# Two linear-attention blocks and two MLPs on one core: layer-norm sums on ScalarE, two denominators' reciprocals on GpSimd, and a reordered start

## The chip, the cores and the metric

The kernel runs on one core of a Trainium2 chip. The core has five engines with instruction streams of their own: TensorE (PE, matmuls; its weight loads, PEld, overlap them), VectorE (DVE), ScalarE (ACT), GpSimd (POOL) and SyncE (SP), which here issues all DMAs. Each engine takes its instructions in order and waits on semaphores for the others. Matmuls write to PSUM, which GpSimd does not read here; all else lies in SBUF. The metric is the device time of one execution in microseconds.

## The reference

Four layers in turn, A, B, A, B, on x of 1 x 2048 x 576 in bfloat16, each with a layer norm ahead and a residual sum behind it. A is linear attention with 32 heads of 18, B an MLP with 4608 hidden units and a layer norm of its own. Both As share one set of weights, and both Bs another.

```python
def _A_ref(x, wqkv, wo):                       # H = 32, Dh = 18
    q, k, v = split(x @ wqkv)
    phi = lambda t: jnp.where(t > 0, t + 1, jnp.exp(t)) + 1e-6
    pq, pk = phi(q), phi(k)
    kv = jnp.einsum("bhsd,bhse->bhde", pk, v)
    z = jnp.einsum("bhsd->bhd", pk)
    num = jnp.einsum("bhqd,bhde->bhqe", pq, kv)
    den = jnp.einsum("bhqd,bhd->bhq", pq, z)[..., None] + 1e-6
    return merge_heads(num / den) @ wo

def _B_ref(x, w1, b1, w2, b2):
    h = _gelu(_layernorm(x) @ w1 + b1)
    return h @ w2 + b2

x = x + _A_ref(_layernorm(x), wqkv, wo)
x = x + _B_ref(_layernorm(x), w1, b1, w2, b2)
x = x + _A_ref(_layernorm(x), wqkv, wo)
x = x + _B_ref(_layernorm(x), w1, b1, w2, b2)
```

## The kernel before

The 2048 tokens are 16 tiles of 128 rows. All weights stay in SBUF. x travels between layers through DRAM (x_d) in float32. The program is written against a framework that places the semaphores and puts each engine's instructions in an order of its own, near that of the program; matmuls are chained by hand (`pe`), and the first tiles' DVE and ACT work too (`chain_on`).

*Layer norm.* Statistics are two `bn_stats` and one `bn_aggr` on DVE (L278 to L284; L804 and L809 for the first tiles), a small DVE operation gives u = var + eps, or for a B layer, whose two norms are folded into one, var (1 + eps) + eps^2 (L289, L292), and GpSimd raises it to -0.5 (L298, L813). The normalized row y goes into a ring of six buffers and is transposed into yT by TensorE or by a transposing DMA (L365). `LNPipe` takes a tile through these stages, one stage at each `tick`.

*Start (`first_tiles`, L788).* Tiles 0 to 5 of the first layer are ordered by hand: rows are fetched (`load_x0`), normalized (0 to 3 on DVE, L820; 4 and 5 on GpSimd, L824 and L826), transposed on TensorE and projected to k (`k_half`). SP issues the transfers in the order of L177 to L187: rows of tiles 0 and 1, the first half of K's weights, tile 2, the second half, tiles 3, 4, 5, then Q's weights and the rest. Later weights are "late pieces", which the k loop issues by a table (`piece_count`, L238): V's weights (`load_wqkv(2)`) and wo come ahead of w1 and w2.

*Layer A, k loop (L523).* For each tile: k projection and phi (`phi_parts`: exp and identity on ACT, min and max on DVE), ky = y^T phi(k) accumulated over all tiles in six PSUM banks (`ky_acc`), and one or two query projections (`q_proj`, one for each of 5 head groups and 4 chunks of 512 tokens, 20 in all, in the order of `q_left`). After the loop: z (L546), kv = Wv^T ky (L558), and kvwo = kv wo by head group (`kv_wo`), with the last six query projections between. The last projection's phi is held back behind kvwo (`late_phi`).

*Layer A, output tiles (L642).* The numerator is never formed alone: phi(q) is scaled by 1/den and multiplied by kvwo. For each chunk `den_stage` forms the 128x128 denominators in PSUM, takes the reciprocal on DVE (L598) and spreads it with a mask into quad_rden (L600); `scale_stage` broadcasts it to the rows of a head group by a matmul (rden_ps, L606), copies it out of PSUM on ACT (rden_bc, L608) and multiplies phi(q) in place on DVE (L609). Chunks 0 and 1 have their denominators ahead of the loop; those of chunks 2 and 3 are formed after tiles 1 and 4. A chunk is scaled during the four tiles ahead of it. `wo_stage` is ten matmuls for each tile into one of two PSUM buffers (wo_ps, accA and accB in turn), and `residual` adds x on DVE (L442) and stores the row (L448); for tiles 2 and 3 ACT copies the matmul's result out (L439) and GpSimd adds (L440). Tiles 0 to 3 are fed to `LNPipe` at once, since the MLP's first chunk needs them: their norm runs on GpSimd (L302, L313, L323), their transposition by DMA.

*Layer B.* For each chunk of 512 tokens: h = gelu(y w1 + b1) (L718 matmuls in pairs on the upper and lower half of the rows, L714 evictions), then four tiles of h w2 (L765), with the norms of the next chunk or layer in between.

Of the kernel before, what the change touches and what calls it, by code (L numbers as in the profile page):

```python
# [15 lines left out]
P = 128  # L16
# [15 lines left out]
C1 = 1.0 + 1e-6  # L32


def build(tc, A_x, A_wqkv, A_wo, B_w1, B_b1, B_w2, B_b2, out, dbg=None, n_layers=4):
    nc = tc.nc
    dbg = dbg or {}
    with ExitStack() as ctx:
# [5 lines left out]
        bank_turn = dict(n=0, both=True)  # L44
# [14 lines left out]
        nc.gpsimd.memset(neg_half[:], -0.5)  # L59
        pow_warm = const.tile([P, 1], F32, name="pow_warm")  # L60
# [117 lines left out]
        load_x0(1)  # L178
        load_wqkv(1, 0)
        load_x0(2)  # L180
        load_wqkv(1, 1)
        load_x0(3)
# [45 lines left out]
        def bias_turn():  # L228
# [6 lines left out]
        late_pieces = [piece_b1_dma, lambda: load_wqkv(2), piece_wo, w1_left[0], w1_left[1], w1_left[2],  # L235
                       lambda: piece_tail(0), w1_left[3], w1_left[4], lambda: piece_tail(1)] + w1_left[5:] + \
                      [(lambda i=i: piece_w2(i)) for i in range(6)]
        piece_count = {4: 1, 5: 2, 6: 1, 7: 2, 8: 1, 9: 1, 12: 2, 14: 3}  # L238
# [6 lines left out]
        class LNPipe:  # L245
# [3 lines left out]
            def feed(self, xt, t, kind, norm_eng, evac_eng="dve", load_from=None, after=None, agg_after=None,  # L249
                     keep=False):  # L250
                xbar = evac_eng == "xbar"
                self.items.append(dict(stage=(0 if load_from is None else -1), xt=xt, t=t, kind=kind,
                                       norm=norm_eng, evac=evac_eng, load=load_from,
                                       after=after, xbar=xbar, agg_after=agg_after, keep=keep))
# [4 lines left out]
            def tick(self, transposes=1):  # L259
                for it in list(self.items):  # L260
# [7 lines left out]
                    if st == -1:  # L268
# [5 lines left out]
                        it["xt"] = xn  # L274
                    elif st == 0:
# [20 lines left out]
                    elif st == 1:  # L296
                        rstd = work.tile([P, 1], F32, name="ln_rstd", bufs=6)
                        nc.gpsimd.tensor_tensor(out=rstd[:], in0=it["u"][:], in1=neg_half[:], op=ALU.pow)  # L298
                        it["rstd"] = rstd
                    elif st == 2 and it["norm"] != "dve":  # L300
                        nmr = work.tile([P, 1], F32, name="ln_nmr", bufs=4)
                        nc.gpsimd.tensor_scalar(out=nmr[:], in0=it["mv"][:, 0:1], scalar1=-1.0,  # L302
                                                scalar2=it["rstd"][:, 0:1], op0=ALU.mult, op1=ALU.mult)
                        it["nmr"] = nmr
                    elif st in (2, 3):
                        y = y_ring[state["ycnt"] % NY]
                        state["ycnt"] += 1
# [125 lines left out]
        def residual(li, t, halves, on_pool=False):  # L433
            xo = xo_of.pop((li, t))
            last = (li == n_layers - 1)
            xn = work.tile([P, D], F32, name="xn", tag="xn", bufs=5)
            res = xn[:, 0:HALF].bitcast(BF16) if last else xn[:]
            if on_pool:
                nc.scalar.copy(out=res.rearrange("p (h n) -> p h n", h=2), in_=halves)  # L439
                nc.gpsimd.tensor_tensor(out=res, in0=res, in1=xo, op=ALU.add)  # L440
            else:
                total = nc.vector.tensor_tensor(out=res.rearrange("p (h n) -> p h n", h=2), in0=halves,  # L442
                                                in1=xo.rearrange("p (h n) -> p h n", h=2), op=ALU.add)
                dve_last["sum"] = total.ins.name
            if last:
                nc.sync.dma_start(out=out_f[t * P:(t + 1) * P, :], in_=res)
                return None
            nc.sync.dma_start(out=x_d[t], in_=xn[:])  # L448
            return xn

        def layer_A(li, next_kind, pre_a1=None, first_tiles=None):
# [62 lines left out]
            if li > 0:  # L514
                for t in range(3):
                    y_load(t)
                begin, q_at = 0, {t: 1 for t in range(14)}
            else:
                first_tiles(k_half, ky_acc)
                begin, q_at = 5, {t: 1 + (t in (12, 14)) for t in range(4, NT)}  # L520
                ky_acc(3, range(KD))
                q_proj(*q_left.pop(0))
            for t in range(begin, NT):  # L523
                if li > 0 and t + 3 < NT:
                    y_load(t + 3)
                k_proj(t, 0)
                if t in q_at and t >= 1:
                    ky_acc(t - 1, range(KD - 1))
                k_proj(t, 1)
                pre_a1(t)  # L530
                if t >= 1:
                    ky_acc(t - 1, (KD - 1,) if t in q_at else range(KD))
                for _ in range(q_at.get(t, 0)):
                    q_proj(*q_left.pop(0))
# [51 lines left out]
            def den_stage(c):  # L586
                dp = bank([P, 512], F32, "den_ps")
                for g in range(G):
                    for j in range(TPC):
                        pe(nc.tensor.matmul(dp[32 * j:32 * (j + 1), 0:P], lhsT=zsel[0:GR[g], g, :],  # L590
                                         rhs=pq[(g, c)][0:GR[g], j * P:(j + 1) * P],
                                         start=(g == 0), stop=False))
                for j in range(TPC):
                    pe(nc.tensor.matmul(dp[32 * j:32 * (j + 1), 0:P], lhsT=eps_row[:], rhs=one_row[:],
                                        start=False, stop=True))
                rden = work.tile([P, P], BF16, name="rden", bufs=1)
                with nc.allow_low_precision("reciprocal of the denominator in the reference's bfloat16"):
                    nc.vector.reciprocal(out=rden[:], in_=dp[:, 0:P])  # L598
                quad = blk.tile([P, D], BF16, name="quad_rden", tag="blk")
                nc.vector.tensor_tensor(out=quad[:, 0:CA].rearrange("p (j n) -> p j n", j=4), in0=quad_mask[:],  # L600
                                        in1=rden[:].unsqueeze(1).to_broadcast([P, 4, P]), op=ALU.mult)
                quad_rden[c] = quad
# [9 lines left out]
            def wo_stage(t):  # L612
                c, j = divmod(t, TPC)
                wp = ps_acc.tile([P, 2, 512], F32, name="wo_ps", tag=("accA", "accB")[t % 2])
                for half in range(2):
                    for g in range(G):
                        pe(nc.tensor.matmul(wp[:, half, 0:HALF], lhsT=pq[(g, c)][0:GR[g], j * P:(j + 1) * P],  # L617
                                              rhs=kvwo[g][0:GR[g], half * HALF:(half + 1) * HALF],
                                              start=(g == 0), stop=(g == G - 1)))
                xn = residual(li, t, wp[:, :, 0:HALF], on_pool=t in (2, 3))  # L620
                if xn is not None and next_kind == "B" and t < TPC:
                    lnp.feed(xn, t, "B", "pool", "xbar")
# [18 lines left out]
            late_phi(after=dve_last["kvwo"], act_after=act_last["kvwo"])  # L641
            for t in range(NT):  # L642
# [3 lines left out]
                wo_stage(t)  # L646
# [9 lines left out]
                if t == NT - 3:  # L656
                    warm_table(ACT.Gelu_apprx_tanh, act_last["copy"])
                lnp.tick()
# [129 lines left out]
        def first_tiles(k_half, ky_acc):  # L788
            ln = {}

            def dve(inst):
                chain_on("dve", inst)
                return inst
# [21 lines left out]
            def norm(t, engine):  # L815
                it = ln[t]
                y = y_of[t] = y_ring[state["ycnt"] % NY]
                state["ycnt"] += 1
                if engine == "dve":
                    dve(nc.vector.tensor_scalar(out=y[:, 0:D], in0=it["x"][:], scalar1=it["mv"][:, 0:1],  # L820
                                                scalar2=it["rstd"][:, 0:1], op0=ALU.subtract, op1=ALU.mult))
                else:
                    nmr = work.tile([P, 1], F32, name="ln_nmr", bufs=4)
                    nc.gpsimd.tensor_scalar(out=nmr[:], in0=it["mv"][:, 0:1], scalar1=-1.0,  # L824
                                            scalar2=it["rstd"][:, 0:1], op0=ALU.mult, op1=ALU.mult)
                    last = nc.gpsimd.tensor_scalar(out=y[:, 0:D], in0=it["x"][:], scalar1=it["rstd"][:, 0:1],  # L826
                                                   scalar2=nmr[:], op0=ALU.mult, op1=ALU.add)
                    pool_last["norm"] = last.ins.name
                del x0_tiles[t]
# [22 lines left out]
            norm(0, "dve")  # L852
# [4 lines left out]
            norm(1, "dve")  # L857
            stats(2, (1,))
            power(2)
            a00, d00 = k_half(0, 0)  # L860
            act(*a00())
            turn(1, False)("dve")
            a01, d01 = k_half(0, 1)
            act(*a01())
            norm(2, "dve")
            a10, d10 = k_half(1, 0)
            stats(3)
            turn(2, True)()
            power(3)
            both(d00())  # L870
            act(*a10())
            a11, d11 = k_half(1, 1)
            act(*a11())
            norm(3, "dve")
# [6 lines left out]
            both(d10())  # L881
# [4 lines left out]
            norm(4, "pool")  # L886
            a30, d30 = k_half(3, 0)
            act(*a30())
            both(d20())
            both(d21())  # L890
# [7 lines left out]
            norm(5, "pool")  # L898
            both(d30())
            both(d31())  # L900
# [21 lines left out]
        for _ in range(4):  # L922
            late_pieces.pop(0)()
# [85 lines left out]
```

## Time and profile before

| | us |
|---|---|
| median of 3 runs (range) | 772.43 (771.15 to 772.85) |
| the profiled execution | 770.18 |
| its span on the core | 768.5 |
| layer 0, first k projection to last output matmul | 6.1 to 106.2 |
| layer 1 (MLP), first matmul to last | 106.2 to 388.1 |
| layer 2, first k projection to last output matmul | 388.1 to 483.1 |
| layer 3 (MLP) and the last store | 483.1 to 768.5 |

How to read the profile: a group has the line of the program, the engine, the operation, written tile <- read tiles, shapes and count, then busy us and the mean ns of one, then how long the engine sat idle just before and what ended that. Positions on the time axis are us from the span's start. A wait names the engine that waited and the instruction whose end released it. In a timeline the figures ahead of an instruction are its start and its duration. "PE busy" counts matmuls from the first to the modelled end, so that back-to-back matmuls of 288 columns show 286 ns each but start every 123 ns.

### The profile page before, as it was taken

How to read it: one execution, taken by the hardware profiler on the slowest of the kernel's cores; microseconds unless marked ns; L12 is line 12 of the kernel's file. 1: busy time of each engine (PE TensorE's matmuls, PEld its weight loads, DVE VectorE, ACT ScalarE, POOL GpSimd, SP SyncE). 2: the span in 40 equal slices, each digit the busy share in tenths (PEclk: the TensorE clock that was granted, in tenths of full speed). 3: DMA queues.
4: the chain of work that ended last, by engine and by line, in shares of the span. 5: the costliest groups of instructions: out<-in, count | busy, mean ns of one | idle time of the engine just before them, and what ended most of it. 6: DMA issues, size and time to landing. Idle time of an engine off the chain costs nothing.

```text
span 768.5 us, 15502 instructions
## 1 busy us (share of the span) xinstructions
PE 755.3 (98%) x6402; PEld 480.4 (63%) x6410; DVE 247.3 (32%) x651; ACT 317.9 (41%) x705; POOL 124.0 (16%) x216
## 2 busy tenths in 40 slices
PE   8999899999999999999999999999999999999998
PEld 4766554675477457646776666447745764674476
DVE  7886952125013402301244589462000000000000
ACT  4667546304600750263056674560065026205600
POOL 3670511013000301200100005321010010011000
PEclk9999999999999999999999999999999999999999
DMA  8979584027113703400431039672100110011000
GB/s 246 216 193 334 149 257 96 28 77 148 35 48 97 142 1 81 126 8 17 133 87 47 9 105 262 212 168 71 49 16 2 32 62 1 25 32 39 2 28 20
DMA packets 82865, 71.13 MB, mean 93 GB/s; under 512 B 44970, under 2 KB 67434, under 8 KB 82794
## 3 DMA queue, kind: packets, MB, share of 16 engines
q1 hardware_dynamic: 82794, 70.14, 33.9%
q8 instruction: 50, 0.82, 0.4%
q14 instruction: 21, 0.17, 0.1%
HBM read 41.74 MB, written 18.87 MB: 79 GB/s over the span
## 4 chain that ended last, share of the span: by engine, by line
PE 93%; DVE 3%; DMA 1%; POOL 1%; issue 1%; ACT 1%; SPq 0%; DVEq 0%; POOLq 0%
PE m_ps L765 37%; PE h_ps L718 20%; PE hp_ps L718 16%; PE q_ps L502 5%; PE ky_ps L491 5%; PE k_ps L461 5%; PE wo_ps L617 4%; DVE pq L609 1%; PE rden_ps L606 1%; DMA x_d<-xn 1%; DMA x<-in_A_x_dram 1%; DVE xn L442 0%; PE kv_ps L558 0%; POOL xn L440 0%; DVE kvwo L580 0%
## 5 line engine op out<-in xcount | busy, mean ns | idle before, releaser
L765 PE MATMUL m_ps<-w_sb,hT 128*128 128x288 bf16 x2304 | 283.6, 286 | 0.0
L765 PEld LDWEIGHTS <-hT 128*128 128x128 bf16 x2304 | 224.8, 98 | 59.8 <-issue 3.4
L718 PEld LDWEIGHTS <-w_sb 64*128 64x128 bf16 x2304 | 124.4, 94 | 136.6 <-issue 1.9
L718 PE MATMUL hp_ps<-yT,w_sb 64*128 64x512 bf16 x1152 | 178.0, 376 | 0.0
L442 DVE TENSOR_TENSOR xn<-m_ps,x_ring 128x576 f32<-128x576 f32 (+1 forms) x32 | 24.2, 758 | 415.4 <-PE m_ps L765 415.4
L718 PE MATMUL h_ps<-yT,w_sb 64*128 64x512 bf16 x1152 | 147.9, 376 | 0.0
L723 ACT COPY relay_sb<-relay_sb 128x1 f32<-128x1 f32 x144 | 28.5, 198 | 264.9 <-PE h_ps L718 222.6
L714 ACT ACTIVATE hT<-h_ps,b1T 128x512 bf16<-128x512 f32 x144 | 91.0, 683 | 44.5 <-PE h_ps L718 44.5
L714 ACT ACTIVATE hT<-hp_ps,b1T 128x512 bf16<-128x512 f32 x144 | 91.1, 692 | 0.0
L426 POOL TENSOR_TENSOR x_ring<-x_ring,b_bc 128x576 f32<-128x576 f32 x32 | 40.7, 1275 | 245.8 <-DMA x_ring<-x_d 243.0
L298 POOL TENSOR_TENSOR ln_rstd<-ln_u,neg_half 128x1 f32<-128x1 f32 x58 | 32.4, 559 | 294.1 <-DVE ln_u L289 201.8
L718 PE MATMUL h_ps<-yT,w_tail 64*128 64x512 bf16 x144 | 54.1, 376 | 0.0
L718 PE MATMUL hp_ps<-yT,w_tail 64*128 64x512 bf16 x144 | 54.1, 376 | 0.0
L461 PE MATMUL k_ps<-wqkv_sb,yT 128*128 128x288 bf16 x320 | 49.2, 286 | 0.9 <-ACT phi_a L396 0.6
L491 PE MATMUL ky_ps<-pk,y_ring 128*128 128x192 bf16 (+5 forms) x318 | 48.7, 285 | 0.5 <-ACT phi_a L396 0.2
L502 PE MATMUL q_ps<-yT,wqkv_sb 128*126 128x512 bf16 (+1 forms) x200 | 48.9, 379 | 0.1
L617 PE MATMUL wo_ps<-kvwo,pq 126*128 126x288 bf16 (+1 forms) x320 | 44.1, 286 | 5.0 <-DVE pq L609 3.1
L393 ACT ACTIVATE phi_e<-k_ps 128x288 bf16<-128x288 f32 x64 | 26.5, 413 | 50.9 <-PE k_ps L461 50.6
L617 PEld LDWEIGHTS <-pq 126*128 126x128 bf16 (+1 forms) x320 | 30.1, 97 | 17.8 <-DVE pq L609 5.1
L461 PEld LDWEIGHTS <-yT 128*128 128x128 bf16 x320 | 30.8, 98 | 14.2 <-issue 1.9
L718 PEld LDWEIGHTS <-w_tail 64*128 64x128 bf16 x288 | 27.1, 94 | 17.1
L400 DVE TENSOR_SCALAR phi_e<-phi_e 128x288 bf16<-128x288 bf16 (+2 forms) x104 | 28.5, 274 | 27.1 <-ACT phi_e L393 26.7
(102 smaller groups left out, 482.7 us busy)
## 6 DMA issues: line engine op xcount, KB each, us to landing
x_ring<-x_d SPq DMA_DIRECT2D x66, 288.0 KB, 3.1
x_d<-xn SPq DMA_DIRECT2D x48, 288.0 KB, 2.6
w_sb<-in_B_w_dram SPq DMA_DIRECT2D x6, 864.0 KB, 10.2
w_sb<-in_B_w_dram SPq DMA_DIRECT2D x9, 512.0 KB, 4.8
x<-in_A_x_dram SPq DMA_DIRECT2D x16, 144.0 KB, 3.6
x_ring<-in_A_x_dram SPq DMA_DIRECT2D x16, 144.0 KB, 3.0
y_d<-y_ring SPq DMA_DIRECT2D x16, 144.0 KB, 1.8
y_ring<-y_d SPq DMA_DIRECT2D x16, 144.0 KB, 2.2
```

What stands on the lines that cost most here:

```text
L298: nc.gpsimd.tensor_tensor(out=rstd[:], in0=it["u"][:], in1=neg_half[:], op=ALU.pow)
L393: exp = nc.scalar.activation(out=e[0:rows, 0:n], in_=ps_ap, func=ACT.Exp)
L400: low = nc.vector.tensor_scalar(out=e[0:rows, 0:n], in0=e[0:rows, 0:n], scalar1=1.0, scalar2=1e-6, op0=ALU.min, op1=ALU.add)
L426: nc.gpsimd.tensor_tensor(out=xo, in0=xo, in1=b2_bc[:], op=ALU.add)
L461: pe(nc.tensor.matmul(kp[:, 0:HALF], lhsT=yT[:, k, tok], rhs=wqkv_sb[:, k, D + half * HALF: D + (half + 1) * HALF], start=(k == 0), stop=( ...
L491: pe(nc.tensor.matmul(ky[at // 512][:, at % 512:at % 512 + n], lhsT=y_of[t][:, c * P:(c + 1) * P], rhs=pk_tiles[t][:, d:d + n], start=(t = ...
L502: pe(nc.tensor.matmul(qp[0:GR[g], :], lhsT=wqkv_sb[:, k, GO[g]:GO[g] + GR[g]], rhs=yT[:, k, c * CA:(c + 1) * CA], start=(k == 0), stop=(k ...
L617: pe(nc.tensor.matmul(wp[:, half, 0:HALF], lhsT=pq[(g, c)][0:GR[g], j * P:(j + 1) * P], rhs=kvwo[g][0:GR[g], half * HALF:(half + 1) * HALF ...
L714: act_last["gelu"] = nc.scalar.activation(out=hT[f][:, 0:CB], in_=dst[n], func=ACT.Gelu_apprx_tanh, bias=b1T[:, f:f + 1], scale=1.0).ins.name
L718: mm = pe(nc.tensor.matmul(dst[n], lhsT=wt, rhs=mv, start=(seen[n] == 0), stop=(seen[n] == 8)))
L723: relay = nc.scalar.copy(out=relay_sb[:, 1:2], in_=relay_sb[:, 0:1])
L765: pe(nc.tensor.matmul(acc[:, half, 0:HALF], lhsT=hT[f][:, j * P:(j + 1) * P], rhs=w2_sb[:, f, half * HALF:(half + 1) * HALF], start=(f == ...
```

## The change

- *Start:* tile 2's rows are fetched ahead of K's weights, tile 3's ahead of their second half. All of tiles 0 to 5 are normalized on DVE, and the DVE, ACT and k-projection steps of the first tiles are set in another order.
- *Late pieces:* w1's first seven column blocks and its tails come first, then V's weights, wo and b1, then the rest.
- *Query projections:* in layer 0 one tile (13) has two of them instead of two tiles (12 and 14), in layer 2 tile 13 has none; in both layers the last one is issued after `late_phi`, just ahead of the output tiles. The ky matmuls are split around the k projection by whether the tile before had a query projection.
- *Residual:* all sums run on DVE; the way over ACT and GpSimd is gone.
- *Statistics of output tiles 0 to 3:* two ACT passes with a running sum take the place of `bn_stats`: Identity with scale -ROOT/D gives minus the mean (times ROOT), Square with that as bias gives the variance. u then comes from GpSimd. These tiles are fed one tile later.
- *Denominators of chunks 2 and 3:* ACT copies them from PSUM to SBUF in float32, and GpSimd raises the 128x128 tile to -1.

The framework's order of the changed kernel differs in the same places; DVE's row among the output tiles becomes: sum 0, phi, sum 1, four scalings of chunk 1, quad_rden of chunk 2, sum 2, last scaling of chunk 1, sums 3 and 4, two scalings of chunk 2, sum 5, quad_rden of chunk 3, scaling, sum 6, two scalings, sums 7 and 8. GpSimd's becomes: power of chunk 2, norms of tiles 0, 1 and 2, power of chunk 3, norm of tile 3.

```diff
+ROOT = D ** -0.5
...
-        bank_turn = dict(n=0, both=True)
+        bank_turn = dict(n=1, both=True)
...
+        minus_one = const.tile([P, 1], F32, name="minus_one")
+        nc.gpsimd.memset(minus_one[:], -1.0)
...
         load_x0(0)
         load_x0(1)
+        load_x0(2)
         load_wqkv(1, 0)
-        load_x0(2)
+        load_x0(3)
         load_wqkv(1, 1)
-        load_x0(3)
...
-        late_pieces = [piece_b1_dma, lambda: load_wqkv(2), piece_wo, w1_left[0], w1_left[1], w1_left[2],
-                       lambda: piece_tail(0), w1_left[3], w1_left[4], lambda: piece_tail(1)] + w1_left[5:] + \
+        late_pieces = w1_left[0:5] + [lambda: piece_tail(0), lambda: piece_tail(1)] + w1_left[5:7] + \
+                      [lambda: load_wqkv(2), piece_wo, piece_b1_dma] + w1_left[7:] + \
                       [(lambda i=i: piece_w2(i)) for i in range(6)]
-        piece_count = {4: 1, 5: 2, 6: 1, 7: 2, 8: 1, 9: 1, 12: 2, 14: 3}
+        piece_count = {4: 1, 5: 1, 6: 1, 7: 2, 8: 1, 9: 1, 12: 2, 13: 1, 14: 3}
...
+                    elif st == 0 and it["stat"] == "act":
+                        xt = it["xt"]
+                        y = it["y"] = y_ring[state["ycnt"] % NY]
+                        state["ycnt"] += 1
+                        mv = work.tile([P, 2], F32, name="ln_mv", bufs=6)
+                        nc.scalar.activation(out=y[:, 0:D], in_=xt[:, 0:D], func=ACT.Identity, scale=-ROOT / D,
+                                             accum_out=mv[:, 0:1])
+                        nc.scalar.activation(out=y[:, 0:D], in_=xt[:, 0:D], func=ACT.Square, scale=ROOT,
+                                             bias=mv[:, 0:1], accum_out=mv[:, 1:2])
+                        it["mv"] = mv
...
                     elif st == 1:
+                        if it["stat"] == "act":
+                            it["u"] = work.tile([P, 1], F32, name="ln_u", bufs=4)
+                            nc.gpsimd.tensor_scalar(out=it["u"][:], in0=it["mv"][:, 1:2], scalar1=1.0 + EPS,
+                                                    scalar2=EPS * EPS, op0=ALU.mult, op1=ALU.add)
...
-        def residual(li, t, halves, on_pool=False):
+        def residual(li, t, halves):
...
-            if on_pool:
-                nc.scalar.copy(out=res.rearrange("p (h n) -> p h n", h=2), in_=halves)
-                nc.gpsimd.tensor_tensor(out=res, in0=res, in1=xo, op=ALU.add)
-            else:
...
-                begin, q_at = 0, {t: 1 for t in range(14)}
+                begin, q_at = 0, {t: 1 for t in range(13)}
...
-                begin, q_at = 5, {t: 1 + (t in (12, 14)) for t in range(4, NT)}
+                begin, q_at = 5, {t: 1 + (t == 13) for t in range(4, NT)}
...
-                if t in q_at and t >= 1:
+                apart = t - 1 in q_at
+                if apart:
                     ky_acc(t - 1, range(KD - 1))
...
-                    nc.vector.reciprocal(out=rden[:], in_=dp[:, 0:P])
+                    if c < 2:
+                        nc.vector.reciprocal(out=rden[:], in_=dp[:, 0:P])
+                    else:
+                        den = blk.tile([P, D], BF16, name="den", tag="blk")[:, 0:2 * P].bitcast(F32)
+                        nc.scalar.copy(out=den, in_=dp[:, 0:P])
+                        nc.gpsimd.tensor_tensor(out=rden[:], in0=den, in1=minus_one[:].to_broadcast([P, P]), op=ALU.pow)
...
-                xn = residual(li, t, wp[:, :, 0:HALF], on_pool=t in (2, 3))
-                if xn is not None and next_kind == "B" and t < TPC:
-                    lnp.feed(xn, t, "B", "pool", "xbar")
+                xn = residual(li, t, wp[:, :, 0:HALF])
+                return xn
...
             late_phi(after=dve_last["kvwo"], act_after=act_last["kvwo"])
+            q_proj(*q_left.pop(0))
+            rows_of = {}
...
-                wo_stage(t)
+                rows_of[t] = wo_stage(t)
...
+                if 1 <= t <= TPC and next_kind == "B":
+                    lnp.feed(rows_of[t - 1], t - 1, "B", "pool", "xbar", stat="act")
                 lnp.tick()
...
-            norm(4, "pool")
...
+            norm(4)
...
-        for _ in range(4):
+        for _ in range(2):
             late_pieces.pop(0)()
```

## The prediction

> **What bounds the kernel now.** I read the shares of the span first, then the engines' busy time by stage, TensorE's waits, and the timelines of the two stretches that are not full.
>
> ```profile
> span 768.5 us, 15502 instructions
> PE 755.3 (98%) x6402; PEld 480.4 (63%) x6410; DVE 247.3 (32%) x651; ACT 317.9 (41%) x705; POOL 124.0 (16%) x216
> PE 93%; DVE 3%; DMA 1%; POOL 1%; issue 1%; ACT 1%; SPq 0%; DVEq 0%; POOLq 0%
> ```
>
> TensorE (PE) is busy 98% and holds 93% of the chain that ended last, so the reader should look only for what fills or opens PE's 13 idle us. By stage (columns: window, its length, then each engine's busy us; layer 0 ends near 106, layer 2 runs from 388 to 483):
>
> ```profile
> 75.00:80.00 5.00, 4.13 (x23) 2.30 (x24) 4.90 (x12) 4.86 (x10) 0.00 (x0) 1.00 0.16 55
> 80.00:106.20 26.20, 24.37 (x218) 16.75 (x221) 22.69 (x50) 10.97 (x20) 11.00 (x18) 1.00 0.78 218
> 106.20:388.00 281.80, 281.80 (x2450) 175.16 (x2450) 64.69 (x151) 99.01 (x218) 38.18 (x61) 1.00 0.32 79
> 458.00:483.00 25.00, 23.14 (x210) 16.18 (x210) 22.09 (x48) 10.84 (x19) 11.24 (x18) 1.00 0.86 261
> ```
>
> The MLP layers have no idle PE at all, at a granted clock of 1.00; nothing in the change can shorten them. VectorE (DVE, third pair) is all but full just where PE is not: 4.90 of 5 us before the output tiles, 22.69 of 26.2 during them. TensorE's waits say on what (us in total, times, longest):
>
> ```profile
> PE wo_ps L617 <- DVE pq L609: 3.1, 2, 1.6
> PE wo_ps L617 <- DVE kvwo L580: 1.6, 2, 0.8
> PE tp L836 <- POOL y_ring L826: 0.7, 1, 0.7
> ```
>
> Both first lines occur once in each attention layer. In layer 0's timeline (start, us, instruction):
>
> ```profile
> 79.00 1.58 PE L617 MATMUL wo_ps<-kvwo,pq 126*128 126x288 bf16 x10 [0.78 <-DVE kvwo L580]
> 85.50 0.87 DVE L600 TENSOR_TENSOR quad_rden<-quad_mask,rden 128x512 bf16<-128x512 bf16 x1
> 86.43 2.68 POOL L440 TENSOR_TENSOR xn<-xn,x_ring 128x576 f32<-128x576 f32 x2
> 86.67 1.31 DVE L609 TENSOR_TENSOR pq<-pq,rden_bc 72x512 bf16<-72x512 bf16 x1
> 88.04 0.91 PE L617 MATMUL wo_ps<-kvwo,pq 72*128 72x288 bf16 x6 [1.52 <-DVE pq L609]
> ```
>
> The scaling at 86.67 takes 1.31 us where its like takes 0.42 (L609 at 83.99), because GpSimd's add runs from 86.43; the quad_rden product takes 0.87 instead of 0.42 beside the normalization on GpSimd from 85.28. A two-input DVE operation stands still until the GpSimd instruction is over. The Trainium skill's page "SBUF — State Buffer" says this as a rule: the port pair that VectorE and GpSimd share is locked for a whole instruction, and the loser waits it out; the trace agrees. By that rule a long GpSimd instruction would also hold every such DVE operation; here none is due during it, as the order below shows.
>
> **The change, part by part.**
>
> *Start-up.* Tile 2's rows are fetched two weight transfers earlier (issue 2.79 becomes about 1.66), tiles 4 and 5 are normalized on DVE (L820, 0.43 us) instead of GpSimd (0.26 + 0.82 plus gaps: 15.47 to 16.66). PE's waits there are 0.59 (tile 1's norm, behind the late rows), 0.72 (tile 4's norm) and 0.24. In the best case all 1.5 go. In the worst the first K weights, issued one row transfer (0.43) later, reach the first projection 0.3 late. I take -0.7: tile 4's wait goes; tile 1's is mostly handed to tile 2, whose norm came at 8.97 behind its GpSimd power and now stands behind two phi operations as well.
>
> *Weights of V and wo later.* They now follow seven pieces of w1, issued about 52 to 54 instead of 14 to 16. They are needed at 69.3 (kv_ps) and 72.6 (kvwo_ps); the same sizes took 5.8 us to land, the slowest weights 10.2. Some 7 us of cover hide it: 0.
>
> *One query projection moved.* From the k loop into the wait before the first output tile. It is 5 x 0.2155 = 1.08 us and the hole 0.78, so that tile starts 0.78 earlier in each layer; in layer 0 one of two steps with a double projection goes, which each ran 4.86 - 3.53 - 1.08 = 0.25 over. Together -1.03 (layer 0) and -0.78 (layer 2). The bounds are 0 (ACT, at 4.86 of 5, holds its phi up) and -1.3.
>
> *The output tiles.* Per layer this takes from DVE two reciprocals (0.95 each) and four tiles' statistics (2 x 0.45 + 0.20 + 0.15 = 1.25), from GpSimd two adds (1.34 each), from ACT two copies (0.64). It adds on DVE two sums (0.75); on ACT eight passes over 128x576 with a running sum (not in this trace; 0.64 is the copy of such a tile, 1.0 the 128x1024 cast of L539; I take 0.72) and two den copies (about 0.3); on GpSimd four small ops (0.26) and two powers over 128x128. PE gets nothing new, so all depends on order. In the changed kernel's instruction order DVE holds, in this row: four scalings of chunk 1, quad_rden of chunk 2 (waits for the power), sum of tile 2, last scaling of chunk 1, sums of tiles 3 and 4, two scalings of chunk 2, sum of tile 5, quad_rden of chunk 3 (waits for the second power), and the rest. So the power does not run beside slack: tile 4's matmuls need sum 2 (two PSUM buffers) and the last scaling, and both are queued behind it.
>
> With P for one power, counted from the first output matmul: it and the ACT chain (sum 0 at 1.35 to 2.1, one statistics pass, four rden copies at 0.52, den copy 0.3) let the first power start at 5.35; quad_rden 0.42 and sum 2 0.76 put tile 4 at 6.7 + P. Before, tile 4 ended at 88.95 - 79.00 = 9.95; now at 6.7 + P + 1.23 = 7.95 + P. GpSimd then holds three normalizations ahead of the second power, each 0.26 + 0.55 + 0.26 + 0.82 + 0.30 and gaps = 2.5, so that starts at 5.35 + P + 7.5 and not when its input is there, some 2.2 earlier. Behind it stand quad_rden, a scaling and sum 6 (0.42 + 0.42 + 0.75), and tile 8 (1.23 plus 0.2) ends at 15.9 + 2P. Before it ended at 96.09 - 79.00 = 17.1 (layer 2: 17.3). So each layer changes by 2P - 1.2 and 2P - 1.4. Tiles 9 to 15 are PE's pace as before, and the last normalization is done 2.5 us after the second power, with eight tiles (about 11 us) before the MLP needs it.
>
> *The price of P.* No power wider than 128x1 is in the trace. The nearest rows on GpSimd (line, form, count, busy us, mean ns):
>
> ```profile
> L426 POOL TENSOR_TENSOR x_ring<-x_ring,b_bc 128x576 f32<-128x576 f32 x32 | 40.7, 1275 | 245.8 <-DMA x_ring<-x_d 243.0 <-DVE ln_st L279 2.8
> L298 POOL TENSOR_TENSOR ln_rstd<-ln_u,neg_half 128x1 f32<-128x1 f32 x58 | 32.4, 559 | 294.1 <-DVE ln_u L289 201.8 <-DVE ln_u L292 92.2
> L824 POOL TENSOR_SCALAR ln_nmr<-ln_mv,ln_rstd 128x1 f32<-128x1 f32 x2 | 0.5, 264 | 0.2
> ```
>
> Lower end: the power's 0.56 stays and 127 more columns go at the add's 1275/576 = 2.2 ns: 0.84 us. Upper end: the power's surplus over a plain 128x1 operation, 0.56 - 0.26 = 0.30, is paid for each of 128 columns: 0.26 + 38 = 38.7 us. The row that is the same operation (L298) says that one column costs 0.30 more than arithmetic, so the add's pace is unlikely; but part of that is paid once and columns may overlap. With ends this far apart I take their geometric middle, sqrt(0.84 x 38.7) = 5.7 us, that is 0.04 us a column.
>
> **The sum.** -0.7 - 1.03 - 0.78 - 1.2 - 1.4 + 4P = 4P - 5.1; with 5.7 it is +17.7. The profiled execution (770.18 us, span 768.5) would become 787.9. It is 2.2 below the shown median of 772.43, to which the same difference gives 790. Break-even is P = 1.28.
>
> **Rivals.** (A) The power streams like the add, P = 0.84: 4 x 0.84 - 5.1 = -1.7, or 770.7, faster. For it: the three other removals are real and DVE is what is full. Against: the 0.30 surplus of a single column. It decides at P = 1.28, and counts up to about 1.7. The Trainium skill's "GPSIMD Engine Reference", section "Performance versus the Vector engine", would have it so for two-input arithmetic: about 2.6 cycles an element at 1.2 GHz, by which an estimate of P is 0.56 + 0.28 = 0.84; the add row's 2.2 ns agrees with that page, and no row shows whether it holds for a power. (B) Columns do not overlap, P from 21 to 38.7: at the end +149.7, or 922. For it: the 0.30. Against: in one instruction some of that is surely paid once. (C) The power is as forecast but PE is not held, since chunk 2's scaled rows are due only after tile 4: then some 2.5 us of each power lie hidden, 17.7 - 10 = +7.7, or 780. Against: sum 2 and the last scaling stand behind quad_rden on DVE, and an engine takes its queue in order.
>
> **How the numbers follow.** Forecast (P between 1.7 and 21, PE held): 0.66, with its own range 774 to 851; A 0.15; B 0.12; C 0.07. The range 771 to 851 leaves out B and the faster part of A, about 2 in 10. This kernel's measurement can tell 0.2%, 1.5 us: faster means P under 0.9, 0.08; the same up to 1.66, 0.08; slower all the rest, 0.84.
>
> **What would show it.** The rows of the 128x128 power on GpSimd give P at once. If the steps hold, the waits list PE wo_ps behind DVE xn (or pq) in four places, two in each attention layer, each near P - 1 us, with DVE idle before quad_rden and GpSimd as releaser, and GpSimd without gaps between its first power and its second; the wait on kvwo is gone, and so is the one of tile 4's transposes; MLP stretches of 281.8 us are as before. I am wrong if P is under 1.3, if PE runs through tile 4 while the power is on, or if a new wait on a weight transfer stands before kv_ps.

## The result and the profile after

| | before | after |
|---|---|---|
| median (range), 4 runs each | 772.19 (771.15 to 772.85) | 851.92 (851.10 to 852.41) |
| span of the profiled execution | 768.5 | 849.8 |
| mean granted clock of TensorE | 1.00 | 0.949 |

The changed kernel takes 1.1033 times as long, with a 95% interval of 1.1014 to 1.1052: some 80 us more. The head of its profile page and the row of the clock that the throttle granted, by slices of a fortieth of the span:

```profile
span 849.8 us, 15505 instructions
...
PE 762.2 (90%) x6406; PEld 484.1 (57%) x6410; DVE 238.7 (28%) x621; ACT 327.9 (39%) x737; POOL 201.8 (24%) x221
...
PEclk9999567999999999999999995599999999999999
```

TensorE's share fell from 98% to 90%, while its busy time rose by 7 us although it has only four matmul records more. GpSimd's busy time rose by 78. The clock row says where: the fives mark two places, one in each attention layer. GpSimd's costliest new group (line, form, count, busy us, mean ns) and TensorE's longest wait (us in total, times, longest):

```profile
L621 POOL TENSOR_TENSOR rden<-den,minus_one 128x128 bf16<-128x128 f32 x4 | 83.1, 20786 | 63.0 <-ACT den L620 63.0
```

```profile
PE wo_ps L640 <- DVE xn L459: 80.9, 4, 20.5
```

One power over 128x128 takes 20.8 us. There are four of them, and four waits of TensorE together nearly as long. The timeline of layer 0 (start, us, instruction; the rows of three engines in order of time) shows how the one leads to the other:

```profile
76.90 1.44 PE L640 MATMUL wo_ps<-kvwo,pq 126*128 126x288 bf16 x10
...
82.13 20.83 POOL L621 TENSOR_TENSOR rden<-den,minus_one 128x128 bf16<-128x128 f32 x1 [28.03 <-ACT den L620]
...
102.99 0.43 DVE L623 TENSOR_TENSOR quad_rden<-quad_mask,rden 128x512 bf16<-128x512 bf16 x1 [20.65 <-POOL rden L621]
...
104.14 2.56 PE L640 MATMUL wo_ps<-kvwo,pq 126*128 126x288 bf16 x10 [20.25 <-DVE xn L459]
...
110.93 20.75 POOL L621 TENSOR_TENSOR rden<-den,minus_one 128x128 bf16<-128x128 f32 x1
...
133.20 2.56 PE L640 MATMUL wo_ps<-kvwo,pq 126*128 126x288 bf16 x10 [20.48 <-DVE xn L459]
...
136.40 2.46 PE L640 MATMUL wo_ps<-kvwo,pq 126*128 126x288 bf16 x10
```

DVE sits idle for 20.65 us ahead of quad_rden, released by GpSimd. TensorE names sum 2 (xn, L459) as its releaser, because that sum stands behind quad_rden in DVE's queue: the name in the wait is the last link, and the cause is one row further up. The second power has no idle time in brackets: GpSimd came to it straight from its three normalizations. The tile behind each wait takes 2.56 us instead of 1.39. By stage (window, length, busy us of PE, PEld, DVE, ACT, POOL, then granted clock, DMA share, GB/s):

```profile
84.00:104.10 20.10, 0.00 (x0) 0.00 (x0) 1.11 (x3) 0.70 (x2) 19.92 (x3) 0.58 0.00 0
...
133.20:147.07 13.87, 13.87 (x86) 9.19 (x87) 8.69 (x16) 4.22 (x7) 1.44 (x3) 0.81 0.57 195
147.07:428.90 281.83, 281.83 (x2450) 175.33 (x2450) 64.69 (x151) 98.98 (x218) 38.28 (x61) 1.00 0.31 79
```

In the first window GpSimd works nearly alone. In the second TensorE is full again, but at a mean clock of 0.81. The MLP lasts 281.8 us as before.

### The profile page after: what moved, and what is told of

It is laid out like the page before. It is cut to its first block, busy times and chain, and to the rows that moved or that the text cites. A ratio compares the mean times of both kernels' runs of the same rounds, so it can differ in the third digit from the quotient of the medians.

```text
span 849.8 us, 15505 instructions
## 1 busy us (share of the span) xinstructions
PE 762.2 (90%) x6406; PEld 484.1 (57%) x6410; DVE 238.7 (28%) x621; ACT 327.9 (39%) x737; POOL 201.8 (24%) x221
## 5 line engine op out<-in xcount | busy, mean ns | idle before, releaser
L459 DVE TENSOR_TENSOR xn<-m_ps,x_ring 128x576 f32<-128x576 f32 (+1 forms) x32 | 24.3, 758 | 415.0 <-PE m_ps L791 415.0
L640 PE MATMUL wo_ps<-kvwo,pq 126*128 126x288 bf16 (+1 forms) x320 | 49.6, 311 | 80.9 <-DVE xn L459 80.9
L447 POOL TENSOR_TENSOR x_ring<-x_ring,b_bc 128x576 f32<-128x576 f32 x32 | 40.7, 1277 | 247.8 <-DMA x_ring<-x_d 242.8
L621 POOL TENSOR_TENSOR rden<-den,minus_one 128x128 bf16<-128x128 f32 x4 | 83.1, 20786 | 63.0 <-ACT den L620 63.0
L640 PEld LDWEIGHTS <-pq 126*128 126x128 bf16 (+1 forms) x320 | 32.9, 104 | 96.1 <-issue 82.8
L631 ACT CAST rden_bc<-rden_ps 126x512 bf16<-126x512 f32 (+1 forms) x40 | 21.4, 588 | 55.4 <-PE rden_ps L629 55.1
```

Of the source, the lines that this page charges most:

```text
L447: nc.gpsimd.tensor_tensor(out=xo, in0=xo, in1=b2_bc[:], op=ALU.add)
L621: nc.gpsimd.tensor_tensor(out=rden[:], in0=den, in1=minus_one[:].to_broadcast([P, P]), op=ALU.pow)
```

## The experiments

Each kernel ran beside the kernel before on the same chip; a ratio is against that. The questions were: what the price of a power consists of, whether TensorE's wait follows it one to one, whether the order on DVE or that on GpSimd sets the wait, what the low clock adds, and what the rest of the change is worth.

**1. The power by itself.** Powers of several shapes and one product on GpSimd are appended to the kernel before, after its last work. Their results are not used, and the time of the whole (824.27 us, one run) is not a comparison.

```diff
+            for n in (2, 8, 32, 64, 128):
+                nc.gpsimd.tensor_tensor(out=low[:, 0:n], in0=src[:, 0:n], in1=minus_one[:].to_broadcast([P, n]),
+                                        op=ALU.pow)
+            nc.gpsimd.tensor_tensor(out=low[0:32, 0:P], in0=src[0:32, 0:P],
+                                    in1=minus_one[0:32, :].to_broadcast([32, P]), op=ALU.pow)
...
+            nc.gpsimd.tensor_tensor(out=low[:, 0:120], in0=src[:, 0:120], in1=minus_one[:].to_broadcast([P, 120]),
+                                    op=ALU.mult)
```

> The kernel before with nine extra GpSimd operations behind its last sum (rows on a constant 3.0, results unused); its time is longer by what they take and is not compared. Theory (each column costs the same, nothing overlaps; 20.8 us for 128 columns and 0.55 for one give 0.159 us a column): 128x2 0.7, 128x8 1.7, 128x32 5.5, 128x64 10.6, 128x128 20.8, 32x128 20.8 (columns count, not partitions), 128x100 to -0.5 in float32 16.3, product 128x120 about 0.5. Rival 1 (the cost is by elements): 32x128 takes 5 us. Rival 2 (the cost hangs on the values or the exponent): 128x128 of the constant is far from 20.8, or 128x100 is not 0.78 of it. Rival 3 (a step with size, as for a buffer): the column price jumps between two of the sizes.

The groups by line of that run (form, count, busy us, mean ns, idle before):

```profile
L953 POOL TENSOR_TENSOR x_ring<-x_ring,minus_one 128x128 bf16<-128x128 f32 x1 | 20.7, 20725 | 0.1
L955 POOL TENSOR_TENSOR x_ring<-x_ring,minus_one 32x128 bf16<-32x128 f32 x1 | 20.7, 20705 | 0.1
...
L953 POOL TENSOR_TENSOR x_ring<-x_ring,minus_one 128x64 bf16<-128x64 f32 x1 | 10.5, 10518 | 0.1
...
L953 POOL TENSOR_TENSOR x_ring<-x_ring,minus_one 128x2 bf16<-128x2 f32 x1 | 0.7, 706 | 0.1
...
L959 POOL TENSOR_TENSOR x_ring<-x_ring,minus_one 128x120 bf16<-128x120 f32 x1 | 0.4, 386 | 0.1
```

From 2 to 128 columns the time grows by 20725 - 706 ns over 126 columns, 0.159 us each, and 0.39 us remains that is paid once. Width 64 by that line is 10.56 (measured 10.52), width 1 is 0.55 (the 128x1 powers of the kernel take 0.56). A quarter of the partitions costs the same. The exponent -0.5 over 128x100 took 16.31, on the line too. A product over 120 columns with the same broadcast operand took 0.386 us in all. So it is the power that is dear, column by column, and neither the broadcast operand nor a wide instruction as such.

**2. The powers taken out.** All reciprocals go back to DVE; all else of the change stays.

```diff
-                    if c < 2:
+                    if c < NCA:
                         nc.vector.reciprocal(out=rden[:], in_=dp[:, 0:P])
```

> The changed kernel with all four chunks' reciprocals on DVE again; all else as changed. Theory (the power is the whole loss, everything else in the change is a gain): PE's four waits of 20 us behind DVE's sum go; the output tiles start 2.1 us (layer 0) and 1.5 us (layer 2) earlier than before, as in the changed kernel's trace, and tiles 0 to 8 run near PE's pace, 14.8 instead of 17.2 us each layer: 772.2 - 3.6 - 4.8 = 764, range 762 to 767. Rival 1 (my prediction's terms without the power, 4 x 0.6 - 5.1): 769.5. Rival 2 (the rest of the change loses too, by the ACT passes with running sums or by the later weights): 772 or more.

Measured: 763.01 us, ratio 0.9895 (0.9879 to 0.9910), clock 0.999. As expected, and faster than both kernels. TensorE's wait on DVE and the window from the first output tile to the MLP in layer 0, in that run:

```profile
PE wo_ps L640 <- DVE xn L459: 0.3, 2, 0.2
```

```profile
76.96:102.46 25.50, 25.23 (x225) 17.45 (x225) 20.53 (x41) 17.13 (x38) 9.52 (x20) 1.00 0.85 270
```

The stretch takes 25.5 us (27.2 before), TensorE is busy for 25.23 of it, and DVE has room. With the reciprocals on DVE there is thus next to nothing left that taking them from DVE could win there: TensorE's waits on DVE's sums are 0.3 us in the whole kernel.

**3. The rest of the change, split.** One kernel has the start, the late pieces and the query projections alone (the statistics, sums and reciprocals are those of before); the other is the kernel of experiment 2 (kernel 2 from here on) with the statistics of tiles 0 to 3 on DVE again, fed at their own tile.

```diff
-                if 1 <= t <= TPC and next_kind == "B":
-                    lnp.feed(rows_of[t - 1], t - 1, "B", "pool", "xbar", stat="act")
+                if t < TPC and next_kind == "B":
+                    lnp.feed(rows_of[t], t, "B", "pool", "xbar")
```

> The kernel before with only the new start, the new order of late weights and the moved query projections; statistics, sums and reciprocals of the output tiles as before. Theory: the output tiles start 2.1 and 1.5 us earlier and then run as before: 772.2 - 3.6 = 768.6, range 767.5 to 770. Rival 1 (the moved projection's phi holds ACT and DVE up and the tiles give it back): 771 to 772. Rival 2 (the prediction's -0.7 -1.03 -0.78): 769.7.

> As e1 (all reciprocals on DVE), and the statistics of output tiles 0 to 3 on DVE again, fed at their own tile; the sums stay on DVE. Theory: DVE is the engine that is full, so its 4 x 1.25 us of statistics in each layer come back into the way of the scalings: about half shows, 767 to 769, that is 3 to 5 above e1 and near e6. Rival (the sums on ACT and GpSimd were the loss, and the statistics fit into DVE's gaps): within 1 us of e1.

Measured: 767.21 us (0.9950, 0.9938 to 0.9963) and 765.45 us (0.9927, 0.9915 to 0.9940). Beside 771.37 for the kernel before, on the same chip as kernel 2, that is a chain of steps: start, pieces and queries -4.2; the sums of tiles 2 and 3 on DVE -1.8; the ACT statistics -2.4; 8.4 in all. The second kernel's expectation was missed from both sides: neither did it fall back to the first, nor did it stay within 1 us of kernel 2. The waits of the first of the two say what the other steps remove:

```profile
PE wo_ps L621 <- DVE pq L613: 3.1, 2, 1.7
...
PE wo_ps L621 <- DVE xn L445: 0.9, 1, 0.9
```

These 4.0 us are 2.6 in the second kernel and 0.3 in kernel 2, and 767.21 - 763.01 is 4.2.

**4. The powers alone.** In the kernel before, only the ACT copy and the power of chunks 2 and 3 are put in.

```diff
+        minus_one = const.tile([P, 1], F32, name="minus_one")
+        nc.gpsimd.memset(minus_one[:], -1.0)
...
-                    nc.vector.reciprocal(out=rden[:], in_=dp[:, 0:P])
+                    if c < 2:
+                        nc.vector.reciprocal(out=rden[:], in_=dp[:, 0:P])
+                    else:
+                        den = blk.tile([P, D], BF16, name="den", tag="blk")[:, 0:2 * P].bitcast(F32)
+                        nc.scalar.copy(out=den, in_=dp[:, 0:P])
+                        nc.gpsimd.tensor_tensor(out=rden[:], in0=den, in1=minus_one[:].to_broadcast([P, P]), op=ALU.pow)
```

> The kernel before with only the den copy and the power for chunks 2 and 3; start, statistics and sums as before. Theory: each of the four powers lengthens the path by 20.8 + 0.3 - 0.95 = 20.1, less the 1.5 us that PE waited at tile 4 anyway, and the low clock behind each wait adds about 2: 772.2 + 80.6 - 3 + 8 = 858, range 852 to 862. Rival (the new statistics on ACT and GpSimd are what holds the second power up, by 2 us a layer): 848 or less.

Measured: 860.89 us, ratio 1.1157 (1.1137 to 1.1176), 88.9 above the 772.00 of the kernel before on its chip. From kernel 2 to the changed kernel the same edit costs 851.92 - 763.01 = 88.9; these two ran on different chips, and with each against the kernel before on its own chip it is 79.7 + 8.4 = 88.1. The loss comes from the powers whatever stands around them; they need no help from the moved statistics and sums.

**5. Half a power.** The power over 64 of the 128 columns, DVE's reciprocal over the others, in the changed kernel.

```diff
+                        n = P // 2
...
+                        nc.vector.reciprocal(out=rden[:, n:P], in_=dp[:, n:P])
+                        nc.gpsimd.tensor_tensor(out=rden[:, 0:n], in0=den, in1=minus_one[:].to_broadcast([P, n]),
+                                                op=ALU.pow)
```

> The changed kernel with GpSimd's power over 64 of the 128 columns of each denominator tile; the other 64 are a DVE reciprocal from PSUM. Theory (the power lies on the path with its whole length, four times): it falls from 20.8 to about 10.5, 851.9 - 4 x 10.3 = 810.7, range 807 to 814. Rival 1 (a part of the power is hidden, so that half of it is hidden more): under 800. Rival 2 (what costs is not the length but the wait as such, PE's clock after it): 830 or more.

Measured: 813.39 us, ratio 1.0532 (1.0514 to 1.0551); one power 10.6 us:

```profile
L623 POOL TENSOR_TENSOR rden<-den,minus_one 128x64 bf16<-128x64 f32 x4 | 42.4, 10605 | 62.2 <-ACT den L621 62.2
```

The time falls by 38.5 where the four powers shrink by 4 x (20.79 - 10.61) = 40.7: TensorE pays for them nearly one to one.

**6. The order on DVE.** The quad_rden products of chunks 2 and 3 are placed behind the sums of tiles 4 and 8, so that tile 4 doesn't wait for a power.

```diff
+                    if c >= 2:
+                        tc.add_manual_dep(prod.ins, dve_last["sum"], NOSYNC, reason="after the sums")
...
+                if t in (4, 8):
+                    quad_rden[1 + t // 4]()
```

> The changed kernel with quad_rden of chunks 2 and 3 put behind the sums of tiles 4 and 8 in DVE's queue (before, ahead of sums 2 and 6). Theory (PE is held by DVE's order, and the second power starts only when GpSimd has done three norms): PE runs through tile 4, the second power starts no earlier after the first, and only tile 8 with its sums comes out from behind the second: 2 to 3 us a layer, 851.9 - 5 = 847, range 844 to 849. Rival 1 (the prediction's rival C, 2.5 us of each power can lie hidden): 842. Rival 2 (the order is no cause): 851 to 853.

Measured: 852.48 us, ratio 1.1046 (1.1030 to 1.1063): nothing won. TensorE's wait moved to the next place that needs the product, and GpSimd's second power starts later (113.65, after 110.93):

```profile
PE rden_ps L638 <- DVE quad_rden L624: 80.3, 4, 22.6
```

```profile
113.65 20.75 POOL L621 TENSOR_TENSOR rden<-den,minus_one 128x128 bf16<-128x128 f32 x1
```

The number is the rival's, but the test isn't clean: in this kernel GpSimd had four normalizations ahead of the second power instead of three, and so lost what tile 4 had gained. What it does show is that DVE's order alone does not free the time while two powers and the normalizations between them stand in one queue.

The same trace answers a question that the prediction left at a rule, namely whether a long GpSimd instruction holds every DVE operation with two inputs in SBUF. Here a scaling became due during the first power:

```profile
82.36 20.83 POOL L621 TENSOR_TENSOR rden<-den,minus_one 128x128 bf16<-128x128 f32 x1 [28.03 <-ACT den L620]
...
84.19 0.42 DVE L641 TENSOR_TENSOR pq<-pq,rden_bc 72x512 bf16<-72x512 bf16 x1 [0.74 <-ACT rden_bc L640]
```

It took its usual 0.42 us, and so did its like in layer 2. The standstills that the prediction read beside an add and a normalization, 1.31 and 0.87 us instead of 0.42, thus don't carry over to a power, which did not hold DVE.

**7. The low clock.** TensorE's tiles behind the waits ran at half pace. To take that away, it is kept busy during the powers by extra matmuls whose results are not used. The first try put 90 of 512 columns ahead of tiles 4 and 8.

```diff
+                if t in (4, 8):
+                    busy_ps = ps_h.tile([P, 512], F32, name="busy_ps", tag="g")
+                    for _ in range(90):
+                        pe(nc.tensor.matmul(busy_ps[:], lhsT=ident[:], rhs=w1_sb[:, 0, 0:512], start=True, stop=True))
                 rows_of[t] = wo_stage(t)
```

> The changed kernel with 90 matmuls of 512 columns on unused data ahead of output tiles 4 and 8 of each attention layer, 19.4 us of the 20.3 that PE waits there. Nothing else is changed. Theory (after each wait PE's granted clock is low for some us: tile 4 takes 2.56 us instead of 1.39): the clock stays at 1.00 and 1.5 to 2.4 us come back at each of the four places, 851.9 - 8 = 844, range 841 to 847. Rival (the slow tiles wait for late operands, not for a clock): 851 to 853, and the tiles still take 2.56.

Measured: 897.63 us, ratio 1.1624 (1.1607 to 1.1642): missed by far, and not for the clock's sake. The framework moved the second quad_rden ahead of sum 5 and a fourth normalization ahead of the second power, so that tile 7 was held and the extra matmuls ahead of tile 8 came behind the wait instead of in it, as pure extra work (21.22 us in layer 0, where those ahead of tile 4 took 19.59):

```profile
113.45 20.75 POOL L621 TENSOR_TENSOR rden<-den,minus_one 128x128 bf16<-128x128 f32 x1
...
135.38 2.56 PE L640 MATMUL wo_ps<-kvwo,pq 126*128 126x288 bf16 x10 [25.61 <-DVE xn L459]
...
137.74 21.22 PE L673 MATMUL busy_ps<-w_sb,ident 128*128 128x512 bf16 x90
```

The next two kernels put them ahead of tile 7 and keep GpSimd's order as in the changed kernel.

```diff
+                            if it["t"] == 3:
+                                tc.add_manual_dep(small.ins, pool_last["pow"], NOSYNC, reason="order as without")
...
+                if t in (4, 7):
...
+                    for _ in range(90):
```

In the second of the two the last line has 106 instead of 90 for tile 7.

> This is the changed kernel with 90 extra matmuls of 512 columns (some 19 us, their output unused) ahead of output tile 4 and of output tile 7 in each attention layer, and with tile 3's statistics kept behind the second power on GpSimd, so that GpSimd's order is the changed kernel's. On DVE the quad_rden product of chunk 3 now stands ahead of sum 5, so that the second wait is tile 7's and not tile 8's; sum 5 and one more scaling then come behind the power, about 0.75 + 0.42 = 1.2 us a layer. Theory (low granted clock after a wait costs about 8 us in all, because TensorE stood still): TensorE is busy during the powers, the granted clock stays at 1.00, the tile after each wait takes about 1.4 us and not 2.56, and the time is 852 - 8 + 2.4 = 846 us (843 to 849). Rival (the low clock costs nothing in the end, since DVE and ACT set the pace of the tiles behind the wait anyway): 852 to 856 us, with the granted clock at 1.00 all the same.

> As the last kernel, with 106 extra matmuls instead of 90 ahead of output tile 7, so that TensorE is busy through the second power too (the last kernel's 90 ended 3.8 us before tile 7 could start, and tiles 7 and 8 then ran at 2.48 us each). Theory (only the low clock behind the second wait of a layer counts: behind the first one GpSimd's small operations set when the second power starts, at 110.9 us in both earlier kernels): tiles 7 and 8 run at 1.4 us, the second power starts near 110.9 as before, and the MLP starts some 2 us earlier in each layer, so 855 - 4 = 851 us (849 to 852.5). Rival (behind the second wait too, DVE and ACT set the pace): 854 to 855.5.

Measured: 854.93 us (1.1079, 1.1050 to 1.1108) and 849.75 us (1.1014, 1.0988 to 1.1039). The first of the two missed the 846 that the theory expected and fell where the rival had put it, though not for the rival's reason: its 90 matmuls ended 3.8 us before tile 7 could start. The second came out as its theory had it (849 to 852.5). The first one's rows of the two waits in layer 0, and of the second power:

```profile
104.03 1.39 PE L643 MATMUL wo_ps<-kvwo,pq 126*128 126x288 bf16 x10 [0.82 <-DVE xn L461]
...
110.94 20.75 POOL L623 TENSOR_TENSOR rden<-den,minus_one 128x128 bf16<-128x128 f32 x1
...
132.88 4.96 PE L643 MATMUL wo_ps<-kvwo,pq 126*128 126x288 bf16 x20 [3.80 <-DVE xn L461]
```

and the row of the second wait with 106 matmuls:

```profile
133.14 2.83 PE L643 MATMUL wo_ps<-kvwo,pq 126*128 126x288 bf16 x20 [0.34 <-DVE xn L461]
```

Two things follow. Behind the first wait the full clock (1.39 instead of 2.56 us) wins nothing: the second power starts at 110.94 as it did at 110.93, since GpSimd comes to it from its own queue. Behind the second wait it counts: two tiles in 2.83 us instead of 4.96, and 849.75 instead of 854.93, at a clock of 1.00. In the changed kernel itself the excess there is 1.2 us (tile 8) plus 1.4 to the end of tile 15 in layer 0, and 1.2 plus 0.65 in layer 2: 4.4 us, where 8 had been expected of it before these runs. The second kernel is no more than some 2 us faster than the changed one because, by the estimate made ahead of experiment 7's last two kernels, its order on DVE puts about 1.2 us a layer behind the second power: 4.4 - 2.4 = 2.0, against 851.92 - 849.75 = 2.2 on two chips.

The Trainium skill's page "TensorE: Matmul & The Clock Gate", section "Part 1: The HAM clock gate", says that the array's clock is halved after an idle window of about 3.4 us and comes back after as long a busy one. These rows agree: 0.34 and 0.82 us of idleness left the tiles at 1.4, 3.8 us brought 2.48, and in the changed kernel the tile at 139.13, 5.9 us behind the wait's end, took 1.40 again.

## Why the prediction failed in size and not in kind

Forecast: 790 us, slower, range 771 to 851. It came out at 851.92, slower, just beyond the range. The step that failed is "The price of P": 5.7 us taken, 20.8 measured. The upper end of the range stood for a P of 21, so a P of 20.8 alone would have left the time inside it, at 772.4 + 78.1 = 850.5; what carried it just beyond is the low clock, a term that the sum didn't have.

- *The formula held.* 4P - 5.1 with P = 20.8 is +78.1; the spans differ by 81.3. Term by term, in us from the two timelines:

| term | by the formula, P = 20.8 | measured |
|---|---|---|
| start and query projection, to layer 0's first output tile | -1.73 | -2.10 |
| query projection in layer 2 | -0.78 | -1.56 |
| first output tile to the end of tile 8, layer 0 | +40.4 | +41.6 |
| the same, layer 2 | +40.2 | +41.3 |
| tiles 9 to 15, layer 0 | 0 | +1.4 |
| tiles 9 to 15, layer 2 | 0 | +0.65 |
| sum | +78.1 | +81.3 |

- *Its inner steps held too.* From the first output tile of layer 0: the first power was put at 5.35 and starts at 5.23; tile 4 was put at 6.7 + P = 27.5 and starts at 27.24; the second power was put at 5.35 + P + 7.5 = 33.65 and starts at 34.03. The four waits were put near P - 1 = 19.8 and are 20.25, 20.48, 20.23 and 19.97. GpSimd has no gap between its powers, the wait on kvwo and the 0.7 us wait of tile 4's transposes are gone, and the MLP has its 281.8.
- *The price.* The bounds were 0.84 and 38.7, and the geometric middle was taken for want of a second width. A middle of ends 46 times apart is no measurement. The nearest row was the same operation on one column: 0.56, 0.30 above plain arithmetic. Of that 0.30 some 0.14 is paid once (0.56 - 0.159 - 0.26), as the prediction allowed; the other 0.159 recurs for every column, and the fall in price that "columns may overlap" stood for did not show at any width from 2 to 128. With all of the 0.30 recurring the row gave 38.7; the measured price is a little over half of that, the one taken about a seventh.
- *What the sum left out.* The low clock behind the waits, 4.4 us by the timelines. With the granted clock at 1.00 all through the profile of before, no term was looked for there; yet each forecast wait of P - 1, 4.7 us at the price taken, left TensorE with nothing to do, and in experiment 7 a wait of 3.8 was enough for slow tiles behind it. The earlier work gained some 1.1 more than forecast (2.10 + 1.56 against 1.73 + 0.78), which hid a quarter of it.
- *The rivals.* A (the power streams like the add, 770.7) fell by a factor of 25 in P. By the Trainium skill's "GPSIMD Engine Reference", section "Performance versus the Vector engine", an estimate was 0.84; its pace agrees with the add (2.2 ns a column) and fits the product here (0.386 us for 120 columns, of which 0.26 by that pace), and does not hold for a power. B (columns don't overlap) has the right mechanism, with 0.159 where it charged 0.30 a column; it was put at P from 21 to 38.7, and the measured 20.8 lies just below its lower edge. C (TensorE not held, 780) fell: the waits are 80.9 of the 83.1 us of powers, and experiment 6, which lets tile 4 run, only moves them.
- *What the other parts were worth.* They make the kernel faster by 8.4 us without the powers (experiment 2). The prediction's -5.1 had these parts and the powers' queue in one sum, so it is not the same figure; it does say that the parts other than the power were seen as gains, and they are.

Left open: whether a power begun some 21 us earlier could be hidden. It wasn't tried. By experiment 2 little could be won by it, since TensorE waits only 0.3 us on DVE's sums with all reciprocals there.

## What to carry to other kernels

Before an operation goes to another engine, find its price per column from two widths; a single narrow instance can't part what is paid once from what recurs, and then the safe reading is that all of it recurs. Relief of a busy engine is worth no more than the waits that name it: here other edits had brought those to 0.3 us, and the move cost some 88. When a forecast makes an engine idle for long, charge the pace at which it comes back, but only at the waits behind which nothing else is late.

## What the runs showed of the hardware

- A power on GpSimd took 0.39 us plus 0.159 us for each column, the same for 32 and 128 partitions, for exponents of -1 and -0.5, and for outputs of two and four bytes. A product of 120 columns took 0.386 us.
- While such a power ran, a DVE product of two SBUF tiles took 0.42 us, as without it (experiment 6).
- TensorE's granted clock was 0.58 over a window of 20.1 us without matmuls. A tile of ten matmuls behind such a wait took 2.56 us, and 1.39 behind a wait of 0.82.
- An ACT pass with a running sum over 128x576 took about 0.7 us (Identity) or 0.8 (Square), and each was followed by a second instruction that reads the sum out, 0.19 to 0.23 us, which the prediction did not count. It did not show in the path: the first power began 5.23 us behind the first output matmul, where 5.35 was put.
